# A prologue in another order, with the pooled values of block 0 as products of their own

## The chip, the cores and the metric

The kernel runs on one core of a Trainium2 chip. The metric is device time in microseconds (us), the median of several executions. The core has five engines with queues of their own: TensorE (PE, its weight loads shown as PEld), VectorE (DVE), ScalarE (ACT), GpSimd (POOL) and SyncE (SP), which here issues all transfers. Each engine works through its instructions in order and waits on semaphores where it needs another's result.

## What is computed

An attention over 4 batches, 8 heads, 768 tokens and 64 dimensions, and behind it a gated feed-forward layer. Every query sees the keys within 15 places of it, and besides them 24 pooled keys, one for each 32 tokens, whose values are means:

```python
k_sum = k.reshape(B, H, nb, block, D).max(axis=3)
v_sum = v.reshape(B, H, nb, block, D).mean(axis=3)
mask_l = np.abs(pos[:, None] - pos[None, :]) < window
scores_s = scale * np.einsum('bhsd,bhnd->bhsn', q, k_sum) + np.log(block)
scores_all = np.concatenate([np.where(mask_l, scores_l, -1e9), scores_s], axis=-1)
a = softmax(scores_all)
x = np.matmul(a, np.concatenate([v, v_sum], axis=2))
g, val = x @ w_gate, x @ w_val
out = (g / (1 + np.exp(-g)) * val) @ w_out
```

Inputs are f32, except that the three weights arrive as 64-bit floats, which the kernel turns into a high and a low f32r part by bit operations.

## The kernel before

*Blocks and units.* The 3072 tokens are cut into 8 blocks of 384 (two per batch). Attention runs per block and unit, a unit being two heads (128 channels), so four units per block. For each it computes scores (`sc`), subtracts the maximum, takes the exponential, normalises (`p`), transposes (`pp`, copied to `pt`) and multiplies by the values (`xo`). Each 64 queries see a window of 96 keys and 24 pooled ones: 120 columns of scores, 120 rows of transposed weights `pt`. The layer behind it runs per block and chunk j of 128 hidden channels, 12 chunks: `gate` and `val` (12 products of 384 columns each, three for each unit: high and low parts), the activation, and `down` (nine products of 512 columns into three accumulators `acc`).

*The prologue.* The string `PROLOGUE` is a program written out by hand: every word is a step with its block, unit or chunk, and behind `=` the engines or PSUM pools that it takes (`a`, `d`, `p` for ACT, DVE, POOL in copies and subtractions; `a`, `b`, `g` for PSUM pools in scores and transposes). It covers the attention of blocks 0 and 1, the turning of all weights and the layer for block 0 and for half of block 1. Behind it a chain of order dependencies holds each engine to the order of the text. The loop for the remaining blocks follows, places fixed by `put_attention`, and its first instruction on each engine except SP is held behind the last of the prologue. On SP a scheduler may place later transfers among the prologue's.

*Steps named below.* `kq` and `q1` load keys and queries, `cst` the constants, `ve`, `vr` and `vo` rows of values into `vrows`, `w_load` weights. `sw` makes the scores of near keys (`a_near`), `sp` those of pooled keys (`a_far`), `pool` the pooled keys `ks`; `ttr`, `exp`, `rcp`, `nrm` are the softmax, `tr` the transposes (`a_turn`), `pt` their copies, `out` the products with the values, `split` and `rest` the two parts of x. Weights go through `w_abs`, `w_c1`, `w_c2`, `w_s1`, `w_s2`, `w_hi`, `w_lo`; activations through `silu`, `mul`, `ah` (high part), `al` (low part).

*Pooled values of the first batch.* `fv` forms partial sums over the value rows in four column strips (`pv`), `fvs` copies them, `fv2` joins them by one product (`pw`), `fvc` copies the 24 joined rows to `vsum["all"]`. `spv(k)` then transfers them from there into rows 96 to 119 of six places of `vrows`, once for block 0 and once for block 1, so that `out` is one product over 120 rows for each head and 64 queries.

*Dummies.* Before the first step three products of zeros run (`WARM`), 4 + 4 + 1 pieces of 128 columns, and at four places `keep(n)` runs one of n pieces into a bank that nobody reads. An f32 product is issued as two instructions, as the counts of the profile show.

Of the kernel before, what the change touches and what calls it, by code (L numbers as in the profile page):

```python
# [78 lines left out]
exp0(0,1) w_abs(0,v) ttr1(0,1) exp1(0,1) q1() sp(0,0) ttr0(0,0) keep(4)=g sw(1,0)=aa kq(2) ttr1(0,0) exp0(0,0)  # L79
w_c1(0,v) w_c2(0,v) w_s1(0,v) rcp(0,1) w_s2(0,v) vr() sp(1,0) nrm(0,1)=p ttr0(1,0) ttr1(1,0) sw(1,1)=bb  # L80
exp1(0,0) rcp(0,0) exp0(1,0) sp(1,1)=h ttr0(1,1) nrm(0,0)=p kq(3) exp1(1,0) ttr1(1,1) sw(0,2)=ab pool(3)
keep(4)=g exp1(1,1) tr0(0,1)=b pt0(0,1)=a sw(0,3)=gb rcp(1,0) pool(2) sp(0,3) tr0(0,0)=g ttr0(0,3) sp(0,2)
nrm(1,0)=p exp0(1,1) rcp(1,1) w_hi(0,v)=d tr1(0,1)=a nrm(1,1)=p ttr0(0,2) ttr1(0,2) exp0(0,3) ve() pt1(0,1)=d
ttr1(0,3) fv()=a exp0(0,2) fvs()=a tr0(1,0)=a pt0(1,0)=d w_load(0,g) w_abs(0,g) w_load(1,gv) sw(1,2)=ab
w_c1(0,g) fv2()=g w_c2(0,g) sp(1,2) tr1(1,0)=b sw(1,3)=ab exp1(0,2) fvc()=a w_s1(0,g) vo(0) rcp(0,2) ttr0(1,2)
w_lo(0,v)=p nrm(0,2)=p w_abs(1,gv) spv(0) pt0(0,0)=d vo(1) pt1(1,0)=a ttr1(1,2) tr0(1,1)=a exp1(0,3) w_s2(0,g)
rcp(0,3) exp1(1,2) nrm(0,3)=p spv(1) sp(1,3)=h w_c1(1,gv) tr1(0,0)=g pt1(0,0)=a tr1(1,1)=a w_hi(0,g)=a
tr0(0,2)=g tr1(0,2)=b w_lo(0,g)=p w_load(2,o) out(0,1)=b ttr0(1,3) ttr1(1,3) pt0(0,2)=d split(0,1)=a pt1(0,2)=a
out(0,0)=g split(0,0)=a exp0(1,2) tr0(0,3)=b tr1(0,3)=a rest(0,1) out(0,2)=b rest(0,0) gate(0,0,0) pt0(0,3)=d
w_load(1,o) gate(0,0,1) w_load(0,o) w_c2(1,gv) val(0,0,0) w_load(2,gv) pt1(0,3)=a out(0,3)=b rcp(1,2) out(1,0)=b  # L90
w_s1(1,gv) exp0(1,3) val(0,0,1) split(0,2)=a rest(0,2) exp1(1,3) split(0,3)=d pt0(1,1)=a w_s2(1,gv) rcp(1,3)
val(0,0,2) pt1(1,1)=a split(1,0)=d rest(0,3) w_hi(1,gv)=a gate(0,0,2) out(1,1)=b nrm(1,2)=p w_abs(0,o)
tr0(1,2)=a rest(1,0) tr1(1,2)=a pt0(1,2)=a pt1(1,2)=d nrm(1,3)=p gate(0,0,3) tr0(1,3)=a tr1(1,3)=b w_c1(0,o)
w_lo(1,gv)=d val(0,0,3) silu(0,0) split(1,1)=a w_c2(0,o) w_s1(0,o) w_load(3,gv) w_abs(2,gv) mul(0,0) w_s2(0,o)
w_abs(1,o) w_c1(1,o) out(1,2)=b w_c1(2,gv) split(1,2)=a pt0(1,3)=a pt1(1,3)=d gate(0,1) w_c2(1,o) val(0,1)
out(1,3)=a room(0) silu(0,1) rest(1,1) w_load(6,o) w_c2(2,gv) w_abs(2,o) gate(1,0,0) mul(0,1) gate(1,0,1)
w_hi(0,o)=a w_abs(3,gv) val(1,0,0) rest(1,2) split(1,3)=a rest(1,3) ah(0,0)=a w_load(4,o) w_load(6,gv)
gate(1,0,2) w_s1(1,o) al(0,0)=d ah(0,1)=a al(0,1)=d w_s2(1,o) w_hi(1,o)=a w_load(3,o) w_c1(2,o) w_lo(0,o)=p
gate(1,0,3) silu(1,0) w_s1(2,gv) w_lo(1,o)=d w_load(4,gv) val(1,0,1) w_load(5,gv) val(1,0,2) val(1,0,3)
w_c2(2,o) w_abs(3,o) w_load(5,o) w_s2(2,gv) down(0,0) mul(1,0) w_c1(3,gv) w_s1(2,o) w_hi(2,gv)=a w_lo(2,gv)=d  # L100
gate(1,1) silu(1,1) w_abs(4,gv) w_c2(3,gv) val(1,1) mul(1,1) w_s1(3,gv) w_load(7,gv) w_s2(3,gv) gate(0,2)
w_c1(3,o) w_c1(4,gv) w_c2(4,gv) w_s1(4,gv) down(0,1) ah(1,1)=a al(1,1)=p gate(1,2) ah(1,0)=a al(1,0)=p down(1,0)
w_s2(2,o) w_abs(5,o) w_load(10,gv) w_hi(3,gv)=a w_lo(3,gv)=d w_c2(3,o) silu(0,2) w_hi(2,o)=a w_lo(2,o)=d
val(1,2) w_c1(5,o) w_s2(4,gv) silu(1,2) mul(1,2) val(0,2) mul(0,2) down(1,1) w_hi(4,gv)=a w_lo(4,gv)=d
w_abs(5,gv) w_c1(5,gv) ah(0,2)=a al(0,2)=d val(1,3) w_c2(5,gv) w_s1(3,o) gate(1,3) w_s2(3,o) w_load(8,o)
w_s1(5,gv) down(0,2) ah(1,2)=a w_abs(6,gv) w_c1(6,gv) w_load(9,gv) silu(1,3) mul(1,3) al(1,2)=d w_hi(3,o)=a
w_abs(4,o) gate(0,3) w_lo(3,o)=d w_load(10,o) w_c2(6,gv) w_abs(6,o) w_s2(5,gv) ah(1,3)=a al(1,3)=d w_s1(6,gv)
w_s2(6,gv) w_c2(5,o) w_c1(6,o) w_c1(4,o) silu(0,3) w_s1(5,o) gate(1,4) silu(1,4) w_hi(5,gv)=a w_hi(6,gv)=a
w_c2(4,o) w_s1(4,o) w_lo(5,gv)=d down(1,2) w_s2(4,o) w_s2(5,o) val(0,3) mul(0,3) w_c2(6,o) w_abs(9,gv)
w_c1(9,gv) val(1,4) mul(1,4) w_hi(5,o)=a w_lo(5,o)=d ah(0,3)=a w_hi(4,o)=a w_s1(6,o) down(1,3) w_lo(4,o)=d  # L110
w_abs(8,o) w_c2(9,gv) al(0,3)=p w_s2(6,o) w_lo(6,gv)=d w_s1(9,gv) gate(0,4) w_c1(8,o) ah(1,4)=d val(0,4)
silu(0,4) mul(0,4) down(0,3) w_hi(6,o)=d w_abs(7,gv) al(1,4)=d w_s2(9,gv) gate(0,5) val(0,5) w_hi(9,gv)=a
down(1,4) w_c2(8,o) w_c1(7,gv) ah(0,4)=a w_load(7,o) w_c2(7,gv) w_load(8,gv) al(0,4)=p silu(0,5) mul(0,5)
ah(0,5)=a w_s1(7,gv) w_s1(8,o) gate(0,6) w_s2(7,gv) w_lo(9,gv)=d val(0,6) w_hi(7,gv)=a w_lo(7,gv)=d al(0,5)=d
silu(0,6) w_abs(8,gv) w_s2(8,o) w_c1(8,gv) w_c2(8,gv) gate(1,5) w_abs(10,gv) silu(1,5) w_c1(10,gv) down(0,4)
mul(0,6) w_load(9,o) val(1,5) ah(0,6)=d down(0,5) w_c2(10,gv) w_s1(10,gv) w_lo(6,o)=d w_hi(8,o)=a w_abs(7,o)
w_lo(8,o)=p w_s2(10,gv) w_abs(10,o) w_abs(9,o) w_hi(10,gv)=a w_s1(8,gv) mul(1,5) w_c1(10,o) w_c1(9,o) w_c1(7,o)
w_c2(10,o) gate(0,7) al(0,6)=p w_c2(7,o) down(0,6) w_s1(10,o) ah(1,5)=a silu(0,7) w_s2(8,gv) val(0,7)
w_hi(8,gv)=a mul(0,7) w_s1(7,o) w_lo(8,gv)=d w_s2(7,o) w_c2(9,o) w_lo(10,gv)=d al(1,5)=p gate(0,9) silu(0,9)
down(1,5) w_s1(9,o) room(1) gate(0,8) ah(0,7)=a al(0,7)=d w_load(11,g) w_hi(7,o)=a w_s2(9,o) w_load(11,v)  # L120
silu(0,8) val(0,8) w_lo(7,o)=d mul(0,8) w_abs(11,g) down(0,7) w_s2(10,o) w_hi(10,o)=d val(0,9) ah(0,8)=a
al(0,8)=d down(0,8) w_lo(10,o)=p w_c1(11,g) w_hi(9,o)=d w_lo(9,o)=d w_abs(11,v) w_load(11,o) load(2,0)
w_c2(11,g) w_c1(11,v) w_c2(11,v) w_abs(11,o) w_s1(11,v) mul(0,9) w_s1(11,g) w_s2(11,g) w_s2(11,v) ah(0,9)=a
al(0,9)=d w_hi(11,g)=a gate(0,10) w_hi(11,v)=d w_c1(11,o) val(0,10) w_c2(11,o) down(0,9) w_lo(11,g)=p silu(0,10)
w_lo(11,v)=d w_s1(11,o) mul(0,10) ah(0,10)=d gate(0,11) silu(0,11) val(0,11) w_s2(11,o) al(0,10)=p down(0,10)
w_hi(11,o)=a mul(0,11) w_lo(11,o)=p ah(0,11)=a al(0,11)=d down(0,11)
"""


# [8 lines left out]
def body(ctx, tc, qP, kP, vT, vP, kq, q1, vE, vR, vO, wgv, wo, cst_in, out):  # L138
    nc = tc.nc
# [247 lines left out]
    def a_near(k, u):  # L387
        t = U[k, u]
        t["sc"] = [a_bank(k, u, f"sc{h}", on[h]) for h in range(2)]
        a = k % HALVES * TOK  # L390
        for i in range(NT):
            c, s = divmod(i, 2)
            qs = slice(i * QT, (i + 1) * QT)
            for h in range(2):
# [1 line left out]
                nc.tensor.matmul(
                    t["sc"][h][s * QT : (s + 1) * QT, c * KC : c * KC + KW], t["q"][hs, qs],
                    KT[u][hs, a + i * QT : a + i * QT + KW], start=True, stop=True,
                )

    def a_far(k, u):
        t = U[k, u]
        m = P if on == "h" else QT
        for i in range(TOK // m):
            c, s = divmod(i * m, P)
            for h in range(2):
                hs = slice(h * D, (h + 1) * D)
                nc.tensor.matmul(  # L408
                    t["sc"][h][s : s + m, c * KC + KW : (c + 1) * KC], t["q"][hs, i * m : (i + 1) * m], ksum[u][hs, :],
                    start=True, stop=True,  # L410
                )
# [56 lines left out]
        a_scale(k, u)  # L468

    def a_turn(k, u, g):  # L470
        ps = U[k, u][f"pp{g}"] = a_bank(k, u, f"pp{g}", on or "a")
        for c in range(NT // 2):
            nc.tensor.transpose(ps[:KC, c * P : (c + 1) * P], U[k, u]["p"][:, g * NT // 2 + c, :], id_sb)  # L473

# [123 lines left out]

    stack, vn = {}, {}

    def keep(n):
# [2 lines left out]
        nc.tensor.matmul(t[:, : n * P], warm[:, :P], warm[:, : n * P], start=True, stop=True)  # L604
# [41 lines left out]
    nc.vector.memset(warm, 0.0)
# [131 lines left out]
```

## Time and profile before

| what | us |
|---|---|
| median of 3 runs | 716.59 |
| lowest and highest of them | 716.12, 975.61 |
| the profiled execution | 713.79 |
| its span, first to last instruction | 712.0 |
| TensorE busy | 702.0 |
| VectorE busy | 279.6 |
| ScalarE busy | 309.1 |
| GpSimd busy | 151.3 |

The times in the views are those of the profiled execution, counted from the start of its span. A row of the timeline gives start, duration, engine, line of the code, operation, output and input, shape and count; in brackets stands how long the engine was idle before it and what ended that. `120*64` is the part of TensorE's array that a product uses, rows by columns. The highest of the three runs is a single one far from the other two.

### The profile page before, as it was taken

How to read it: one execution, taken by the hardware profiler on the slowest of the kernel's cores; microseconds unless marked ns; L12 is line 12 of the kernel's file. 1: busy time of each engine (PE TensorE's matmuls, PEld its weight loads, DVE VectorE, ACT ScalarE, POOL GpSimd, SP SyncE). 2: the span in 40 equal slices, each digit the busy share in tenths (PEclk: the TensorE clock that was granted, in tenths of full speed). 3: DMA queues.
4: the chain of work that ended last, by engine and by line, in shares of the span. 5: the costliest groups of instructions: out<-in, count | busy, mean ns of one | idle time of the engine just before them, and what ended most of it. 6: DMA issues, size and time to landing. Idle time of an engine off the chain costs nothing.

```text
span 712.0 us, 12729 instructions
## 1 busy us (share of the span) xinstructions
PE 702.0 (99%) x5106; PEld 638.6 (90%) x5106; DVE 279.6 (39%) x814; ACT 309.1 (43%) x763; POOL 151.3 (21%) x151
## 2 busy tenths in 40 slices
...
GB/s 340 226 377 417 130 1 0 131 75 186 163 169 67 46 43 2 112 46 91 90 58 77 68 46 46 46 72 18 46 46 45 89 17 1 1 45 1 1 1 44
DMA packets 49123, 61.93 MB, mean 87 GB/s; under 512 B 20968, under 2 KB 38120, under 8 KB 47784
## 3 DMA queue, kind: packets, MB, share of 16 engines
...
q8 instruction: 40, 0.66, 0.4%
q14 instruction: 19, 0.16, 0.1%
...
## 4 chain that ended last, share of the span: by engine, by line
PE 94%; ACT 2%; DVE 2%; DMA 1%; issue 0%; POOL 0%; ACTq 0%
PE v L535 29%; PE g L535 28%; PE acc L585 28%; PE xo L500 4%; PE sc L381 3%; PE pp L473 2%; DMA vrows<-vs 1%; PE dummy L604 1%; DVE p L422 1%; ACT p L437 0%; PE pv L348 0%; DVE ks L294 0%; PE pv L330 0%; POOL al L158 0%; ACT L437 0%
## 5 line engine op out<-in xcount | busy, mean ns | idle before, releaser
L535 PE MATMUL v<-xh,w_gv 128*128 128x384 f32 x640 | 179.3, 341 | 0.0
L585 PE MATMUL acc<-w_o,ah 128*128 128x512 f32 x576 | 178.9, 392 | 0.0
L535 PE MATMUL g<-xh,w_gv 128*128 128x384 f32 x640 | 178.6, 340 | 0.0
L158 POOL TENSOR_TENSOR al<-a,ah 128x384 fp32r<-128x384 f32 x84 | 89.3, 1063 | 313.3 <-ACT ah L162 309.7
L546 DVE TENSOR_TENSOR a<-v,a 128x384 f32<-128x384 f32 x96 | 53.4, 556 | 253.9 <-PE v L535 252.8
L585 PEld LDWEIGHTS acc<-w_o,ah 128*128 128x128 f32 x576 | 108.0, 188 | 19.7
L535 PEld LDWEIGHTS v<-xh,w_gv 128*128 128x128 f32 x640 | 117.2, 188 | 3.4 <-issue 2.4
L535 PEld LDWEIGHTS g<-xh,w_gv 128*128 128x128 f32 x640 | 117.3, 188 | 2.6 <-ACT a L541 0.3
L585 PE MATMUL acc<-w_o,al 128*128 128x512 f32 x288 | 113.6, 395 | 0.1
L541 ACT ACTIVATE a<-g 128x384 f32<-128x384 f32 x96 | 47.1, 491 | 143.8 <-PE g L535 142.3
L535 PE MATMUL g<-xl,w_gv 128*128 128x384 f32 x320 | 108.0, 338 | 0.0
L535 PE MATMUL v<-xl,w_gv 128*128 128x384 f32 x320 | 107.9, 337 | 0.0
L162 ACT CAST ah<-a 128x384 fp32r<-128x384 f32 x93 | 47.3, 510 | 112.5 <-DVE a L546 105.4
L437 ACT ACTIVATE p<-p,nm 128x120 f32<-128x120 f32 x192 | 73.2, 383 | 6.9 <-DVE nm L422 6.7
L459 POOL TENSOR_TENSOR p<-p,ri 128x720 f32<-128x720 f32 x32 | 45.8, 1432 | 121.3 <-DVE ri L455 107.1
L585 PEld LDWEIGHTS acc<-w_o,al 128*128 128x128 f32 x288 | 54.0, 188 | 9.9 <-issue 0.5
L535 PEld LDWEIGHTS g<-xl,w_gv 128*128 128x128 f32 x320 | 60.1, 188 | 2.3
L535 PEld LDWEIGHTS v<-xl,w_gv 128*128 128x128 f32 x320 | 60.1, 188 | 0.3
L541 ACT ACT_TABLE_LOAD x25 | 32.1, 1283 | 53.0 <-PE g L535 52.9
L422 DVE CUSTOM_DVE_ANT_0 p<-sc,consts 128x120 f32<-128x120 f32 x192 | 41.3, 277 | 1.7 <-PE sc L408 1.4
L535 PE MATMUL g<-xh,w_g 128*128 128x384 f32 x128 | 36.9, 345 | 0.0
L535 PE MATMUL v<-xh,w_v 128*128 128x384 f32 x128 | 36.6, 343 | 0.0
...
## 6 DMA issues: line engine op xcount, KB each, us to landing
...
```

What stands on the lines that cost most here:

```text
L158: (nc.vector if e == "d" else nc.gpsimd).tensor_tensor(out=out, in0=a, in1=b.bitcast(F32), op=ALU.subtract)
L162: nc.scalar.copy(out, in_)
L381: nc.tensor.matmul(sc[h][s * QT : (s + 1) * QT, c * KC : (c + 1) * KC], t["q"][hs, qs], t["kw"][hs, i, :], start=True, stop=True,)
L422: nc.vector.tensor_tensor_reduce(out=t["p"][:, i, :], in0=t["sc"][g][:, c * KC : (c + 1) * KC], in1=bias_sb[:, 0 if n == 0 else 2 if n == ...
L437: nc.scalar.activation(out=t["p"][:, i, :], in_=t["p"][:, i, :], func=AF.Exp, scale=-1.0, bias=t["nm"][:, i : i + 1], accum_out=t["sm"][:, ...
L459: (nc.vector if on == "d" else nc.gpsimd).tensor_tensor(out=p, in0=p, in1=ri.rearrange("p (n o) -> p n o", o=1).broadcast_to([P, NT, KC]), ...
L473: nc.tensor.transpose(ps[:KC, c * P : (c + 1) * P], U[k, u]["p"][:, g * NT // 2 + c, :], id_sb)
L500: nc.tensor.matmul(ps[hs, qs], vw, t["pt"][:n, h, qs], start=k not in OWN or i == 0, stop=k not in OWN)
L535: nc.tensor.matmul(ps[:, :TOK], w[:, cs], x, start=u == 0 and n == 0, stop=u == NP - 1 and n == 2)
L541: nc.scalar.activation(out=a, in_=A.pop(("g", k, j))[:, :TOK], func=AF.Silu)
L546: nc.vector.tensor_tensor(out=a, in0=ps[:, :TOK], in1=a, op=ALU.mult)
L585: nc.tensor.matmul(ACC[k][i], a[:, ts], w, start=j == 0 and n == 0, stop=j == NJ - 1 and n == 2)
```

## The change

Five things change. (1) `WARM` goes from (4, 4, 1) to (4, 3), into one bank. (2) The `keep` steps go; instead a score step can begin with a product of zeros into its own bank (`zeros`), of as many 128-column pieces as the digit behind its pools says. (3) `OWN = (0,)`: for block 0 `out` multiplies only the 96 rows of near values, in one accumulation, and a new use of `outp` adds the 24 pooled rows as one product of 384 columns per head; `spv(0)` goes. (4) Transfers behind the prologue's are held behind its last one, too. (5) The text of the prologue is written in a new order, with other engines for some copies.

```diff
-WARM = (4, 4, 1)
-OWN = ()
+WARM = (4, 3)
+OWN = (0,)
...
     def a_near(k, u):
...
         t["sc"] = [a_bank(k, u, f"sc{h}", on[h]) for h in range(2)]
+        zeros(t["sc"][0], on[2:])
...
     def a_far(k, u):
         t = U[k, u]
-        m = P if on == "h" else QT
+        m = P if on[:1] == "h" else QT
+        for _ in range(int(on.strip("hq") or 0)):
+            nc.tensor.matmul(t["sc"][0][:, NTP * P :], warm[:, :P], warm[:, :P], start=True, stop=True)
...
     def a_turn(k, u, g):
-        ps = U[k, u][f"pp{g}"] = a_bank(k, u, f"pp{g}", on or "a")
+        ps = U[k, u][f"pp{g}"] = a_bank(k, u, f"pp{g}", on[:1] or "a")
+        zeros(ps, on[1:])
...
-    def keep(n):
-
-        t = a_bank(0, 0, "dummy", on)
-        nc.tensor.matmul(t[:, : n * P], warm[:, :P], warm[:, : n * P], start=True, stop=True)
+    def zeros(t, n):
+
+        if n:
+            nc.tensor.matmul(t[:, : int(n) * P], warm[:, :P], warm[:, : int(n) * P], start=True, stop=True)
...
-        if x.engine in last and x.engine != mybir.EngineType.SP:
+        if x.engine in last:
             after(x, last[x.engine])
```

`a_out` and `a_out_pooled` are in both kernels; before, `OWN` was empty and no step called the second:

```python
n = KW if k in OWN else KC
...
nc.tensor.matmul(ps[hs, qs], vw, t["pt"][:n, h, qs], start=k not in OWN or i == 0, stop=k not in OWN)
...
vw = vsum["all"][KW:, u * P + h * D : u * P + (h + 1) * D]
nc.tensor.matmul(t["xo"][hs, :TOK], vw, t["pt"][KW:, h, :], start=False, stop=True)
```

The first line of the text, before and after. Zero products stand in `sw(0,1)`, `sp(0,1)` and, further on, `sw(0,3)=ga3`: 4, 1 and 3 pieces.

```diff
-kq(1) sw(0,1)=ag keep(2)=a pool(1) kq(0) keep(2)=b cst() pool(0) sp(0,1) sw(0,0)=ga ttr0(0,1) w_load(0,v)
+kq(0) cst() sw(0,0)=bg kq(1) pool(0) q1() w_load(0,g) sp(0,0) ttr0(0,0) exp0(0,0) sw(0,1)=bg4 pool(1) sp(0,1)=h1
```

Over the whole prologue the new text gives DVE 15 `al` instead of 11, 5 `ah` instead of 3, the `fvc` copy, 11 low parts of single weights instead of 9, 5 `pt` instead of 7 and 1 `split` instead of 2.

SyncE's queue before, from the last rows of values on (`vrows<-vs` is a spread, `vw` are value windows of block 2):

```order
L178 DMA raw_gv_426<-in_wgv 128x2048
L630 DMA vrows<-in_vO 128x1536
L286 DMA vw_0_1853<-in_vP 96x6x128
L286 DMA vw_1_1948<-in_vP 96x6x128
L370 DMA vrows<-vs_479 24x6x512
L630 DMA vrows<-in_vO 128x1536
L370 DMA vrows<-vs_479 24x6x512
L178 DMA raw_o_546<-in_wo 128x1024
```

The same place after:

```order
L249 DMA kq_262<-in_kq 128x1184
L627 DMA vrows<-in_vE 128x2x1536
L177 DMA raw_v_409<-in_wgv 128x1024
L633 DMA vrows<-in_vO 128x1536 x2
L177 DMA raw_gv_519<-in_wgv 128x2048
L369 DMA vrows<-vs_521 24x6x512
L177 DMA raw_o_552<-in_wo 128x1024
```

Both rows of `vO` and the first double chunk now stand ahead of the only spread, and the two windows of block 2 have left the place.

TensorE's order before, from the transposes of unit 2 to the first gate product (`xo_1_548` is unit 1 of block 0):

```order
L473 MATMUL pp_0_2_541<-consts,p_2_386 120x128 x3
L500 MATMUL xo_1_548<-pt_1_318,vrows 64x64 x12
L500 MATMUL xo_0_577<-pt_0_497,vrows 64x64 x12
L473 MATMUL pp_0_3_596<-consts,p_3_354 120x128 x3
L473 MATMUL pp_0_3_600<-consts,p_3_354 120x128 x3
L500 MATMUL xo_2_605<-pt_2_571,vrows 64x64 x12
L535 MATMUL g_0_619<-xh_0_590,w_g_535 128x384
```

And after, from the join of the partial sums (`pw`) to the first gate product:

```order
L359 MATMUL pw_0_490<-warm,consts 120x512
L476 MATMUL pp_0_2_502<-consts,p_2_356 120x128 x3
L503 MATMUL xo_0_506<-pt_0_264,vrows 64x64 x12
L511 MATMUL xo_0_506<-pt_0_264,vs_521 64x384 x2
L503 MATMUL xo_1_534<-pt_1_454,vrows 64x64 x12
L476 MATMUL pp_0_2_547<-consts,p_2_356 120x128 x3
L476 MATMUL pp_0_3_568<-consts,p_3_399 120x128 x3
L511 MATMUL xo_1_534<-pt_1_454,vs_521 64x384 x2
L538 MATMUL g_0_578<-xh_0_557,w_g_476 128x384
```

The pooled products of units 0 and 1 (`vs`, 384 columns) have come between, and the first gate product stands ahead of the values of units 2 and 3.

More of the change, by code (lines that the diff above doesn't have):

```diff
@@ L77 @@
 PROLOGUE = """
-kq(1) sw(0,1)=ag keep(2)=a pool(1) kq(0) keep(2)=b cst() pool(0) sp(0,1) sw(0,0)=ga ttr0(0,1) w_load(0,v)
[L79 to L126, printed above, removed]
+kq(0) cst() sw(0,0)=bg kq(1) pool(0) q1() w_load(0,g) sp(0,0) ttr0(0,0) exp0(0,0) sw(0,1)=bg4 pool(1) sp(0,1)=h1
@@ new lines @@
+kq(2) sw(1,0)=aa ttr1(0,0) exp1(0,0) sp(1,0) ttr0(0,1) vr() rcp(0,0) ttr1(0,1) exp0(0,1) sw(1,1)=bb w_abs(0,g)
+ttr0(1,0) ttr1(1,0) sp(1,1)=h nrm(0,0)=p exp1(0,1) tr0(0,0)=g exp0(1,0) kq(3) pt0(0,0)=a exp1(1,0) tr1(0,0)=b
+ttr0(1,1) w_c1(0,g) rcp(0,1) nrm(0,1)=p w_c2(0,g) pool(2) ttr1(1,1) sw(0,2)=gb sw(0,3)=ga3 pool(3) pt1(0,0)=a
+ve() w_s1(0,g) rcp(1,0) sw(1,2)=ab sp(0,2)=h sp(1,2)=h w_s2(0,g) exp0(1,1) ttr0(0,2) ttr1(0,2) exp1(1,1) sp(0,3)
+tr0(0,1)=b tr1(0,1)=g exp0(0,2) nrm(1,0)=p tr0(1,0)=a rcp(1,1) ttr0(0,3) ttr1(0,3) w_load(0,v) vo(0) tr1(1,0)=b
@@ new lines @@
+exp1(0,2) fv()=g ttr0(1,2) exp0(0,3) nrm(1,1)=p tr0(1,1)=a pt0(1,0)=a tr1(1,1)=a rcp(0,2) ttr1(1,2) fvs()=a
+pt0(0,1)=d pt1(0,1)=d vo(1) exp1(0,3) pt1(1,0)=d sw(1,3)=ba w_hi(0,g)=d sp(1,3) fv2()=b rcp(0,3) nrm(0,2)=p
+ttr0(1,3) tr0(0,2)=g out(0,0)=b w_load(1,gv) fvc()=d spv(1) w_abs(0,v) outp(0,0) exp0(1,2) w_c1(0,v) nrm(0,3)=p
+w_c2(0,v) out(0,1)=g tr1(0,2)=b w_lo(0,g)=d w_load(0,o) exp1(1,2) split(0,0)=a pt0(0,2)=a w_abs(1,gv) rcp(1,2)
+rest(0,0) pt1(0,2)=d tr0(0,3)=b ttr1(1,3) outp(0,1) nrm(1,2)=p gate(0,0,0) w_s1(0,v) w_load(1,o) w_c1(1,gv)
@@ new lines @@
+tr1(0,3)=b w_s2(0,v) out(0,2)=b outp(0,2) exp0(1,3) pt0(0,3)=a pt1(0,3)=a out(1,0)=b w_hi(0,v)=a w_c2(1,gv)
+pt0(1,1)=a split(0,2)=d out(0,3)=b rest(0,2) split(0,1)=a outp(0,3) w_load(3,o) w_abs(0,o) pt1(1,1)=a tr0(1,2)=b
+w_load(2,gv) rest(0,1) w_lo(0,v)=p w_s1(1,gv) w_s2(1,gv) val(0,0,0) val(0,0,1) split(1,0)=a out(1,1)=a exp1(1,3)
+rcp(1,3) tr1(1,2)=a gate(0,0,1) split(0,3)=a w_hi(1,gv)=a gate(0,0,2) rest(0,3) rest(1,0) nrm(1,3)=p gate(0,0,3)
+w_load(5,o) val(0,0,2) val(0,0,3) w_c1(0,o) w_c2(0,o) w_lo(1,gv)=d pt0(1,2)=a pt1(1,2)=a tr0(1,3)=b w_s1(0,o)
@@ new lines @@
+w_s2(0,o) silu(0,0) split(1,1)=a w_abs(2,gv) out(1,2)=b tr1(1,3)=a mul(0,0) w_hi(0,o)=a w_load(2,o) w_c1(2,gv)
+rest(1,1) w_lo(0,o)=p ah(0,0)=a pt0(1,3)=a gate(0,1) al(0,0)=p silu(0,1) split(1,2)=a w_load(3,gv) pt1(1,3)=d
+val(0,1) w_c2(2,gv) w_abs(2,o) out(1,3)=b w_abs(1,o) val(1,0,0) mul(0,1) rest(1,2) w_s1(2,gv) w_c1(2,o)
+split(1,3)=a val(1,0,1) rest(1,3) w_c2(2,o) w_load(4,gv) room(0) w_abs(3,gv) gate(1,0,0) gate(1,0,1) val(1,0,2)
+ah(0,1)=a al(0,1)=d val(1,0,3) gate(1,0,2) w_c1(1,o) gate(1,0,3) down(0,0) w_load(7,gv) w_c2(1,o) w_s1(1,o)
@@ new lines @@
+w_abs(3,o) silu(1,0) mul(1,0) w_s2(1,o) ah(1,0)=a gate(1,1) w_c1(3,gv) w_s2(2,gv) w_s1(2,o) w_hi(1,o)=a
+w_load(5,gv) w_lo(1,o)=d w_load(10,gv) w_load(10,o) al(1,0)=d w_hi(2,gv)=a w_s2(2,o) w_c1(3,o) w_c2(3,gv)
+w_lo(2,gv)=d silu(1,1) val(1,1) mul(1,1) w_load(8,gv) w_abs(4,gv) w_hi(2,o)=d down(0,1) w_lo(2,o)=d w_c1(4,gv)
+w_c2(3,o) w_s1(3,gv) w_s2(3,gv) w_s1(3,o) ah(1,1)=a w_load(4,o) gate(0,2) silu(0,2) w_hi(3,gv)=a al(1,1)=d
+w_c2(4,gv) gate(1,2) w_s2(3,o) w_abs(4,o) w_c1(4,o) val(0,2) mul(0,2) silu(1,2) w_abs(10,o) down(1,0)
```

28 lines of the change are left out of this document (25 added, 3 removed).

## The prediction

> **What bounds the kernel now.** I read the page's busy table first, then the stages, then TensorE's timeline and the chain of waits in the first 45 us. In the stages (below the page's two lines) the columns are the stretch, the busy time and instructions of PE, PEld, DVE, ACT and POOL, the granted clock, the DMA share and GB/s.
>
> ```profile
> span 712.0 us, 12729 instructions
> PE 702.0 (99%) x5106; PEld 638.6 (90%) x5106; DVE 279.6 (39%) x814; ACT 309.1 (43%) x763; POOL 151.3 (21%) x151
> ...
> 0.00:10.00 10.00, 7.89 (x107) 5.00 (x108) 4.05 (x20) 2.62 (x8) 0.20 (x4) 1.00 0.79 290
> 10.00:20.00 10.00, 9.17 (x203) 5.77 (x204) 9.51 (x60) 10.00 (x51) 5.06 (x4) 1.00 1.03 409
> 20.00:30.00 10.00, 8.39 (x117) 4.88 (x111) 8.72 (x50) 8.74 (x31) 5.18 (x5) 1.00 0.87 230
> 30.00:40.00 10.00, 8.55 (x138) 7.79 (x139) 6.47 (x13) 5.87 (x25) 3.29 (x2) 0.83 0.66 197
> 40.00:100.00 60.00, 59.91 (x379) 55.80 (x378) 55.73 (x85) 33.49 (x53) 7.13 (x5) 1.00 0.62 255
> 100.00:157.00 57.00, 57.00 (x296) 52.82 (x296) 46.91 (x74) 20.70 (x34) 12.80 (x8) 1.00 0.14 45
> 700.00:712.00 12.00, 8.23 (x42) 7.19 (x40) 2.23 (x4) 1.96 (x4) 0.18 (x1) 1.00 0.18 66
> ```
>
> TensorE sets the time: 702.0 of 712.0 us. Of the 10 us in which it is idle, 6.0 lie in the first 40 us and 3.8 in the last 12, which the change leaves alone. So the end moves by when TensorE starts, by the products added and removed, and by the holes of the first 40 us. Its timeline there (start, duration, what, count, idle time before it and what ended that):
>
> ```profile
> 1.45 4.21 PE L604 MATMUL dummy<-warm 128*128 128x512 f32 x6 [1.45 <-DVE warm L646]
> 5.59 1.16 PE L396 MATMUL sc<-kq 64*64 64x96 f32 x24
> 6.68 1.13 PE L604 MATMUL dummy<-warm 128*128 128x256 f32 x4
> 7.74 0.55 PE L408 MATMUL sc<-ks,kq 64*64 64x24 f32 x24
> 8.11 0.70 PE L396 MATMUL sc<-kq 64*64 64x96 f32 x24
> ...
> 9.79 1.10 PE L604 MATMUL dummy<-warm 128*128 128x512 f32 x2 [0.66 <-DVE nm L422]
> 11.16 0.73 PE L396 MATMUL sc<-kq,q 64*64 64x96 f32 x24 [0.28 <-DMA q<-in_q]
> ...
> 12.66 0.85 PE L408 MATMUL sc<-ks,q 64*128 64x24 f32 x12
> ...
> 14.10 1.12 PE L604 MATMUL dummy<-warm 128*128 128x512 f32 x2
> 15.61 0.52 PE L473 MATMUL pp<-consts,p 128*120 128x128 f32 x3 [0.39 <-DVE nm L422]
> ...
> 19.01 2.88 PE L348 MATMUL pv<-vrows,consts 128*32 128x512 f32 x14
> ...
> 30.83 2.83 PE L500 MATMUL xo<-pt,vrows 120*64 120x64 f32 x48 [2.44 <-DMA vrows<-vs]
> ...
> 34.50 0.92 PE L500 MATMUL xo<-pt,vrows 120*64 120x64 f32 x24
> 35.35 0.44 PE L535 MATMUL g<-xh,w_g 128*128 128x384 f32 x1
> 35.63 0.34 PE L535 MATMUL g<-xl,w_g 128*128 128x384 f32 x1
> ...
> 38.67 0.92 PE L500 MATMUL xo<-pt,vrows 120*64 120x64 f32 x24 [0.62 <-DMA vrows<-vs]
> ```
>
> The holes after the start are 0.66, 0.28, 0.39, 2.44 and 0.62 us: 4.39 together. The last two wait for the transfers that spread the pooled values over the value rows. They are on the chain of waits (first two lines), SyncE holds the weight loads behind them (next three), and behind the first hole the granted clock stands at 0.50 for 3 us (last line, columns as in the stages):
>
> ```profile
> 25.89 4.80 DMA vrows<-vs
> 32.97 5.56 DMA vrows<-vs
> ...
> 11.13 4.01 SPq L286 DMA_DIRECT2D vw<-in_vP  x2
> 25.89 0.98 SPq L370 DMA_DIRECT2D vrows<-vs  x1
> 33.81 2.71 SPq L178 DMA_DIRECT2D raw_o<-in_wo  x3
> ...
> 30.83:33.85 3.02, 3.02 (x49) 2.90 (x50) 1.07 (x2) 1.01 (x3) 0.28 (x1) 0.50 0.28 114
> ```
>
> **The change, part by part.** *Start: -0.94 us.* Nine zero blocks of 128 columns took 4.21 us, seven take 3.27, so the first scores come at 4.72 instead of 5.66. Their keys are there, since the first reduction over keys starts at 4.54:
>
> ```profile
> 4.54 0.95 DVE L294 TENSOR_REDUCE ks<-kq 128x24 f32<-128x768 f32 x1 [3.14 <-DMA kq<-in_kq]
> ```
>
> *Dummies out, zero products in: -3.35 and +2.24.* The dummies behind the start took 1.13 + 1.10 + 1.12 us. The new zero products are 4 + 1 + 3 blocks at 1.12 / 4 = 0.28 each. They run ahead of scores, on TensorE's path.
>
> *Own products for the pooled values: +4.0, from 2.5 to 7.4.* Each unit of block 0 gets two products of 384 columns, over 24 rows and into 64 columns, each issued as two instructions like the other f32 ones. No row has this shape. A full f32 instruction of 512 columns takes 1.12 / 2 = 0.56 us, so one of 384 takes 0.42. Four in a row make 1.68 per unit, with a switch 1.85 (upper end, x4 = 7.4). If the two heads run side by side in the two column halves it is 0.84. The cheapest near row is pv, which uses column strips: 14 instructions of 512 columns in 2.88 us, 0.21 each, hence 4 x 0.21 x 384/512 = 0.62 (lower end, x4 = 2.5). The scores come nearer in kind, 64-wide tiles of both heads in turn: 24 instructions of 96 columns in 0.70 us are 0.029 each, where a full array would take 0.56 x 96/512 = 0.105, so 3.6 of 4 tiles worked at once. I take 0.84 plus 0.16, 1.0 per unit, for switches: the first g behind the 64-wide xo takes 0.44 us and the next 0.34, so one costs 0.10. The remaining products keep their count and width; 96 rows instead of 120 are costed at nothing.
>
> The Trainium skill, TensorEngine Tiling (Array Packing), section Tiling Modes, speaks against these products: a change of tiling mode drains TensorE. The trace agrees as far as its 0.10 us goes. Without any drain the products would come to 4 x 0.84 = 3.4 and the sum below to 0.6 us less.
>
> *Holes: -3.3, and the slow clock: -1.2.* Block 0 waits for no spread any more: -2.44. The second spread (block 1) is issued when the joined sums are copied. Between the join and the first product that needs it TensorE has four pp (0.5 each), three out (0.85), three pooled products (1.0) and a gate piece (0.5): 8.1 us. The copy of 24x512 (0.58 in the row below) and 4.80 to 5.56 of transfer are 6.1 at most: -0.62, with 2 us to spare. The queries of block 1 go ahead of one 512 KB weight, 1.3 us at 409 GB/s, and arrive at 9.9; TensorE is there at 4.72 + 1.16 + 0.55 + 1.12 + 0.70 + 0.28 + 0.85 = 9.4. That is a hole of 0.5, the 0.39 may stay, and of the three small ones (1.33) I leave 1.1. Behind the hole of 2.44 us 48 xo took 2.83 us where 2 x 0.85 was due; the stage at a clock of 0.50 lasted 3.02 us, and I put the loss at 1.2. No hole of such a length is left.
>
> *Transfers.* Block 2's two value windows leave the prologue's queue, 4.01 us of SyncE's time, and come behind block 0's results. They are needed at 172.08, and results leave at 155.60; even the slowest spread above took 5.56 us, so it is hidden, and without that cover TensorE would wait for the difference. Only one spread is left, issued some 2 us after the place of the old first one (25.89), so the weights behind it start at about 28.5 instead of 33.81.
>
> *DVE: +0.4, from 0 to 3.7.* It gets four more low parts of activations (0.55 each), one cast more (0.55 at most), the copy of the pooled values (0.58) and two more low parts of weights (0.73), less two copies of turned weights (0.55): +3.7. That is hidden as long as TensorE is the later one: from 40 us on DVE waits for a product 7.3 us in five waits. But the low part of the third weight chunk ends at 59.32 + 1.22 = 60.54 and block 0's gate with it starts at 61.47 (the g row below), so there the cover is 0.9 us.
>
> ```profile
> L158 DVE TENSOR_TENSOR al<-a,ah 128x384 fp32r<-128x384 f32 x11 | 6.0, 551 | 0.6 <-ACT ah L162 0.6
> L158 DVE TENSOR_TENSOR w_o<-m_o,w_o 128x512 fp32r<-128x512 f32 x8 | 5.8, 728 | 0.0
> L162 ACT COPY vs<-pw 24x512 f32<-24x512 f32 x1 | 0.6, 579 | 0.0
> ...
> DVE a L546 <- PE v L535: 7.3, 5, 2.5
> ...
> 59.32 1.22 DVE L158 TENSOR_TENSOR w_gv<-m_gv,w_gv 128x1024 fp32r<-128x1024 f32 x1
> 61.47 0.34 PE L535 MATMUL g<-xh,w_gv 128*128 128x384 f32 x1
> ...
> 155.60 1.69 SPq L596 DMA_DIRECT2D out<-o  x3
> 172.08 0.96 DVE L164 COPY vw<-vs 24x768 f32<-24x768 f32 x1 [0.16 <-ACT vs L331]
> ```
>
> The sum: -0.94 - 3.35 + 2.24 + 4.0 - 3.3 - 1.2 + 0.4 = -2.15 us. The profiled execution took 713.79 us, 1.8 around its span; it would take 711.6. It lies 2.8 under the median of the runs, 716.59. The forecast is for the median: 714.4 us.
>
> **The rivals.** *The wait moves on* (the change does not do what it says). The first pooled product stands behind one pp and one out (1.35 us) after the join, and needs the copy (0.58), which is now DVE's: 0.8 us to spare. If DVE, in order, comes to that copy 3 us late, a hole of 2.2 us and the slow clock's 1.2 are back: -2.15 + 3.4 = +1.25, 717.8 us. For it: DVE is busy 9.5 and 8.7 of 10 us in the stages from 10 to 30. Against it: its work ahead of the copy is scores that TensorE has long delivered. Chance 0.13.
>
> *The pooled products run one behind the other*: 7.4 in place of 4.0, -2.15 + 3.4 = +1.3, 717.9 us. For it: both heads read the same 24 rows, where the scores' heads read different ones. Against it: pv's strips share their rows too and come to 0.21 us. Chance 0.12.
>
> *DVE takes over, slower than before.* The place is the gate of block 0's third weight chunk. TensorE gets there at about 61.0, 2.5 us sooner by the sum but with a down product of 2.1 us put ahead of it. By the order DVE has 1.4 us more to do before it, against a cover of 0.9. So TensorE waits unless DVE is idle at least 1 us less before than it was: 0.5 + 1.3 + 3.5 us in the stages from 10 to 40. If DVE keeps the lead in time from there on, none of TensorE's gain comes through and the extra work shows in full: 716.6 + 3.7 = 720.3 us. For it: DVE is busy 55.73 of 60 us. Against it: 3.5 of that idle time lies in the stage of the spread's holes, and the weights arrive 5 us sooner. Chance 0.14.
>
> *The slow clock at the start lasts longer.* The first scores take 1.16 us and the next ones 0.70, so the clock comes up at about 6.5 us. If it comes one stage of 3 us later, work of that stage takes twice the time: -2.15 + 1.5 = -0.65, 715.9 us. For it: seven zero blocks instead of nine, then smaller tiles. Against it: TensorE has no hole there before 9.4. Chance 0.08. The Trainium skill, TensorE: Matmul & The Clock Gate, Part 1: The HAM clock gate, has a rule for this: a window of about 3.4 us that runs freely decides, so the moment of the rise varies between executions. The trace has one rise and one fall and agrees with the length, 3.02 us; it can't show the variation.
>
> *Cheaper than reckoned*: pooled products at 2.5, no small hole left: -2.15 - 1.5 - 1.1 - 0.4 = -5.1, 711.5 us. Chance 0.06.
>
> **How the numbers follow.** The forecast has 0.47 and is the predicted time. Its own range is 712 to 717, from 2.5 to 5 for the pooled products and 0 to 1.5 for DVE. The range for 8 in 10 is 710.5 to 719.0: it takes in the cheap case and three of the rivals, and leaves out most of DVE's. Two per cent, 14.3 us, is about what a measurement of this kernel can tell from no change. A gain of that size would need all idle time, all dummies and the start together, so faster gets 0.01. A loss of it needs weights to be late by four times DVE's extra work: 0.03, out of the DVE rival. The rest, 0.96, is within 2%.
>
> **What would show it.** Each step has its row in the changed profile: first scores at 4.7 us; pooled products at 1.0 us per unit; no wait of xo for the spread; no stage at a clock of 0.50 after 7 us; the first gate about 3 us sooner than 35.35; PE busy up by about 2 us and idle time down by 3. The forecast is wrong if TensorE waits for DVE at gates between 40 and 150 us, if the pooled products take 1.7 us per unit, or if a hole of over 2 us opens ahead of them.

## The result, and the profile after

| | us |
|---|---|
| the changed kernel, median of 6 runs | 710.8 (710.54 to 711.5) |
| the kernel before, median of 6 runs | 715.08 (713.18 to 975.61) |
| ratio of the runs, 95% interval | 0.9946 (0.9929 to 0.9964) |
| profiled execution, before and after | 713.79 and 711.5 |
| span, before and after | 712.0 and 709.7 |

The change makes the kernel 0.54% faster, some 4 us by this comparison: clear of noise, and within the 2% for which 0.96 was given. Forecast were 714.4 us, in 710.5 to 719.0. The measured median lies 0.3 us above the lower end of that range. The two profiled executions differ by 2.3 us, where the sum of the prediction said 2.15. Single executions far above the rest, like the 975.61 here, do not enter a ratio.

The page of the changed kernel, then its stages, columns as before:

```profile
span 709.7 us, 12696 instructions
PE 702.5 (99%) x5094; PEld 638.6 (90%) x5094; DVE 281.2 (40%) x820; ACT 308.7 (43%) x763; POOL 140.2 (20%) x145
...
20.00:30.00 10.00, 10.00 (x139) 5.77 (x139) 8.65 (x46) 8.76 (x36) 5.13 (x4) 1.00 0.64 231
30.00:40.00 10.00, 10.00 (x136) 7.54 (x133) 9.05 (x21) 8.29 (x25) 3.07 (x3) 1.00 0.96 355
40.00:100.00 60.00, 60.00 (x360) 56.41 (x360) 55.99 (x89) 30.46 (x47) 3.93 (x3) 1.00 0.52 215
100.00:157.00 57.00, 57.00 (x298) 53.10 (x297) 47.16 (x73) 20.75 (x33) 5.93 (x5) 1.00 0.15 48
157.00:200.00 43.00, 42.19 (x370) 36.52 (x369) 25.61 (x84) 29.04 (x78) 13.04 (x15) 1.00 0.71 204
```

TensorE's busy time rises by 0.5 us and its idle time falls from 10.0 to 7.2. From 16 to 157 us it has no hole at all, and the clock stays at 1.00 where it had been 0.83. One stage is worse: from 157 to 200 us TensorE is idle for 0.81 us, against 0.12 before, as the same stage of the kernel before shows:

```profile
157.00:200.00 43.00, 42.88 (x373) 38.26 (x372) 25.87 (x84) 28.57 (x77) 12.24 (x15) 1.00 0.61 184
```

The timeline of TensorE in the changed kernel, at the places that answer to those shown of before, and with the hole of block 2 at its end:

```profile
4.74 1.24 PE L396 MATMUL sc<-kq 64*64 64x96 f32 x24
5.75 0.80 PE L410 MATMUL sc<-ks,kq 64*64 64x24 f32 x24
6.48 1.49 PE L607 MATMUL sc<-warm 128*128 128x512 f32 x2
8.20 0.73 PE L396 MATMUL sc<-kq 64*64 64x96 f32 x24 [0.23 <-DMA kq<-in_kq]
8.86 0.49 PE L405 MATMUL sc<-warm 128*128 128x128 f32 x2
9.27 0.85 PE L410 MATMUL sc<-ks,kq 64*128 64x24 f32 x12
10.09 0.73 PE L396 MATMUL sc<-kq,q 64*64 64x96 f32 x24
...
12.76 0.87 PE L476 MATMUL pp<-consts,p 128*120 128x128 f32 x6 [0.32 <-DVE nm L424]
...
14.99 0.91 PE L607 MATMUL sc<-warm 128*128 128x384 f32 x2 [0.56 <-ACT pt L161]
...
26.52 0.92 PE L503 MATMUL xo<-pt,vrows 96*64 96x64 f32 x24
27.37 0.86 PE L511 MATMUL xo<-pt,vs 24*64 24x384 f32 x4
28.16 0.92 PE L503 MATMUL xo<-pt,vrows 96*64 96x64 f32 x24
...
30.60 0.44 PE L538 MATMUL g<-xh,w_g 128*128 128x384 f32 x1
...
33.30 1.62 PE L503 MATMUL xo<-pt,vrows 120*64 120x64 f32 x48
...
172.90 0.51 PE L476 MATMUL pp<-consts,p 128*120 128x128 f32 x3 [0.81 <-DVE nm L424]
```

A pooled product starts at 27.37 and the next instruction at 28.16: 0.79 us per unit. The first product that needs a spread (block 1, at 33.30) has no wait before it. SyncE's queue and VectorE's waits show why, and what the hole of block 2 hangs on (timelines; the last line is from the waits from 157 to 200 us, with total, times and longest):

```profile
27.02 0.98 SPq L369 DMA_DIRECT2D vrows<-vs  x1
28.05 2.65 SPq L177 DMA_DIRECT2D raw_o<-in_wo  x3
...
162.35 0.95 DVE L314 TENSOR_REDUCE vr<-vt 128x24 f32<-128x768 f32 x1 [2.48 <-DMA vt<-in_vT]
...
DVE vr L314 <- DMA vt<-in_vT: 3.0, 2, 2.5
```

The spread leaves at 27.02, the weights behind it at 28.05 instead of 33.81. In block 2, values of unit 1 stand behind the queries and key windows of the same unit, which the change has put behind the results; VectorE, in order, waits 2.48 us for them. The chain of waits of this execution leads from that transfer, issued at 156.73, over this reduction and further work of VectorE and ScalarE to the transposes at 172.90.

### The profile page after: what moved, and what is told of

It is laid out like the page before. It is cut to its first block, busy times and chain, and to the rows that moved or that the text cites. A ratio compares the mean times of both kernels' runs of the same rounds, so it can differ in the third digit from the quotient of the medians.

```text
span 709.7 us, 12696 instructions
## 1 busy us (share of the span) xinstructions
PE 702.5 (99%) x5094; PEld 638.6 (90%) x5094; DVE 281.2 (40%) x820; ACT 308.7 (43%) x763; POOL 140.2 (20%) x145
## 4 chain that ended last, share of the span: by engine, by line
PE 94%; DMA 2%; ACT 2%; DVE 1%; SPq 0%; issue 0%
PE v L538 28%; PE g L538 28%; PE acc L588 27%; PE xo L503 4%; PE pp L476 3%; PE sc L380 2%; ACT p L439 1%; DMA kq<-in_kq 1%; DMA vt<-in_vT 1%; PE xo L511 0%; PE pv L347 0%; DVE ks L293 0%; PE sc L410 0%; PE sc L396 0%; PE pv L329 0%
## 5 line engine op out<-in xcount | busy, mean ns | idle before, releaser
L157 POOL TENSOR_TENSOR al<-a,ah 128x384 fp32r<-128x384 f32 x80 | 81.5, 1019 | 300.8 <-ACT ah L161 300.8
```

What stands on the lines that cost most here:

```text
L157: (nc.vector if e == "d" else nc.gpsimd).tensor_tensor(out=out, in0=a, in1=b.bitcast(F32), op=ALU.subtract)
```

## The experiments

Twelve runs in three groups. In each group the kernel before ran on the same chip: medians 713.95, 714.43 and 714.08 us. Times and ratios below are against that. A ratio is worked out from the single executions, so it can differ by 0.1% from the quotient of the two medians. "The changed kernel" is the one of the change; its own second measurement is the fifth run.

### Later transfers free again

```diff
-        if x.engine in last:
+        if x.engine in last and x.engine != mybir.EngineType.SP:
```

> The changed kernel without its fourth part: later transfers may again be placed among the prologue's by the scheduler. Theory (the ledger: every part is worth what its rows show on TensorE's path): the hold costs the one hole that the changed kernel has in block 2, 0.81 us at 172.9, where VectorE had waited 2.48 us for a transfer of values. Freed, queries and windows of unit 1 leave before the results again, the hole closes, and the kernel is 0.5 to 0.8 us faster than the changed one (about 710.1 against 710.8). Rival: the hold is part of the gain, because the two value windows of block 2 now go among the last weights and delay them; then it is the same or slower by up to 1 us.

710.63 us, ratio 0.9958 (0.9943 to 0.9973). The scheduler puts the two value windows among the last weights, and the queries of unit 1 ahead of the results. The hole of block 2 closes to 0.13 us, as the stage of this run shows:

```profile
157.00:200.00 43.00, 42.87 (x408) 37.41 (x406) 26.29 (x86) 29.53 (x79) 13.02 (x15) 1.00 0.58 171
```

In this order, the hole was the hold's doing. Whether the time falls with it, this pair alone does not tell: the intervals of this ratio and the changed kernel's overlap almost wholly. For the rival, a delay by the windows, nothing speaks: they leave at 59.19 us, and the time is no longer.

### Block 0's spread put back

```diff
-OWN = (0,)
+OWN = ()
...
-out(0,0)=b w_load(1,gv) fvc()=d spv(1) w_abs(0,v) outp(0,0)
+w_load(1,gv) fvc()=d spv(0) out(0,0)=b spv(1) w_abs(0,v)
```

The other three `outp` go as well.

> The changed kernel with the pooled values of block 0 spread by a transfer again, in the new order: no own products. Theory: it saves the four pairs of products (4 x 0.79 = 3.2 us) and gets back a hole behind the join, because the copy ends near 27.0 us, a spread takes 4.8 and TensorE has only some 1.3 us of transposes between; hole 3 to 5 us, clock at 0.50 for up to 3.4 us behind it (1 to 1.7 lost). Net 1 to 3.5 us slower than the changed kernel. Rival: the new order alone makes the gain, then this one is as fast as the changed kernel or up to 3 us faster.

715.69 us, ratio 1.002 (1.0011 to 1.0028): 4 to 5 us slower than the changed kernel, and slower than the kernel before. TensorE's wait and the two stages around it in this run:

```profile
31.89 2.83 PE L503 MATMUL xo<-pt,vrows 120*64 120x64 f32 x48 [5.01 <-DMA vrows<-vs]
...
20.00:30.00 10.00, 6.88 (x82) 3.43 (x80) 7.81 (x44) 7.36 (x35) 4.87 (x4) 0.97 0.58 217
30.00:40.00 10.00, 7.44 (x132) 7.01 (x132) 4.94 (x14) 5.23 (x15) 1.35 (x2) 0.69 0.95 305
```

That is more than expected: the hole is 5.01 us, at the top of its range. The clock column gives the time at half clock: what is missing to 1.00, times the length of the stage, times two. Here that is (0.03 + 0.31) x 10 x 2 = 6.8 us, twice the 0.17 x 10 x 2 = 3.4 of the kernel before. With a spread for block 0 at this place, the new order alone is worth less than nothing.

### Without the zero products

```diff
-sw(0,1)=bg4
+sw(0,1)=bg
-sp(0,1)=h1
+sp(0,1)=h
-sw(0,3)=ga3
+sw(0,3)=ga
```

> The changed kernel without its three zero products. Theory: they take 2.7 us on TensorE (1.49, 0.41 and 0.84), but two of them only fill waits: the second keys land at 8.18 in any case, and the bank of the third is free at 14.99. So 0.4 to 1.2 us faster than the changed kernel, the small holes grow to 2.5 us together, and the clock stays at 1.00 after its rise. Rival (the clock needs them): a hole of 1.5 us at 6.5 us keeps the clock at 0.50 for one more stage of 3.4 us, so 0.5 to 1.5 us slower than the changed kernel, with a granted clock below 1.00 in the stage from 7 to 14 us.

712.83 us, ratio 0.9993 (0.9976 to 1.0011): 1.4 to 2.0 us slower than the changed kernel's two medians, 711.43 and 710.8. TensorE's timeline, then the stages of this run:

```profile
7.14 0.72 PE L396 MATMUL sc<-kq 64*64 64x96 f32 x24 [0.85 <-DMA kq<-in_kq]
8.13 0.85 PE L410 MATMUL sc<-ks,kq 64*128 64x24 f32 x12 [0.27 <-DVE ks L293]
9.11 1.15 PE L396 MATMUL sc<-kq,q 64*64 64x96 f32 x24
...
0.00:10.00 10.00, 7.30 (x112) 4.79 (x116) 4.65 (x24) 4.22 (x16) 0.20 (x4) 0.96 0.78 298
10.00:20.00 10.00, 9.95 (x200) 8.70 (x192) 8.53 (x54) 8.86 (x42) 4.47 (x3) 0.70 1.01 407
```

The theory fell, the rival held. Behind two holes of 0.85 and 0.27 us the scores take 1.15 us where they took 0.73, and the clock is at half for 6.8 us ((0.04 + 0.30) x 20). In ten of the twelve executions the mean clock is 0.995 or less. The other two, at 0.999 and 1.000, took 712.91 and 717.68, so the clock does not explain every execution.

### Only the first zero product

The second and the third are taken out as above, `sw(0,1)=bg4` stays.

> The changed kernel without its second and third product of zeros (1 and 3 pieces); the first of 4 pieces stays. Theory: without all three the clock fell because the wait for the second keys lay open within its first full stage; the first product covers that wait, the others only cost their 0.41 and 0.84 us, less what opens as waits. So 0.5 to 1.2 us faster than the changed kernel, clock at 1.00 from its rise on. Rival: the small ones are needed as well, then the clock is at 0.50 for a stage between 6 and 20 us and it is 0.5 to 2 us slower.

714.79 us, ratio 0.9997 (0.9981 to 1.0013); single times from 711.9 to 717.4, but for one far off. That is 3.4 us slower than the changed kernel beside it, 711.43, and more than the rival said. Again the theory fell. In the profile the wait that the third product had stood in lies open, and the clock falls a little later:

```profile
15.56 0.73 PE L396 MATMUL sc<-kq 64*64 64x96 f32 x24 [1.08 <-ACT p L439]
...
10.00:20.00 10.00, 8.31 (x205) 7.36 (x206) 9.63 (x62) 9.94 (x50) 4.46 (x3) 0.89 1.02 403
20.00:30.00 10.00, 10.00 (x109) 5.80 (x107) 6.04 (x39) 6.04 (x27) 3.76 (x3) 0.77 0.53 215
```

The single executions agree: three with a mean clock of 1.000 took 711.9 to 712.6 us, eight with 0.996 or less 712.9 to 717.4. So the products of zeros are paid for by the clock that they keep, the second and third too, which were taken out together; which of these two it needs is not shown.

### The kernel before without its dummies

Every `keep(n)` is taken out of the text.

> The kernel before without its four dummies. Theory of the prediction: they are on TensorE's path, 3.35 us, of which some 1.1 turn into a wait for the queries: 1.5 to 2.5 us faster than before. Rival (from the run without zero products): they keep the clock up, without them it falls to 0.50 for one or two stages in the first 20 us, and the kernel is the same or up to 2 us slower.

716.44 us, ratio 1.0016 (1.0002 to 1.0029): slower by about 1 to 2 us, not faster by 2: the rival held. The wait for the queries lies open, and the clock is at half for 13.6 us ((0.44 + 0.24) x 20):

```profile
11.24 1.33 PE L396 MATMUL sc<-kq,q 64*64 64x96 f32 x24 [3.54 <-DMA q<-in_q]
...
10.00:20.00 10.00, 8.76 (x162) 7.58 (x162) 7.79 (x41) 8.71 (x45) 4.44 (x3) 0.56 1.02 407
20.00:30.00 10.00, 10.00 (x123) 4.47 (x123) 6.04 (x35) 6.09 (x22) 3.17 (x3) 0.76 0.68 189
```

### Own products alone in the kernel before

```diff
-OWN = ()
+OWN = (0,)
```

`spv(0)` goes and each `out(0,u)` is followed by `outp(0,u)`.

> The kernel before with the own products alone: no spread for block 0, each out of block 0 followed by its pooled product; order, dummies and all else as before. Theory: the hole of 2.44 goes with its slow clock (1.2), the hole of 0.62 goes or shrinks, and the products cost 4 x 0.79 = 3.2: about 1 us faster than before (0.5 to 2). Rival (the order is what counts): no gain or slower by up to 1.5 us, because TensorE only runs into the next wait of the old order, for transposed weights or weights of the layer.

713.0 us, ratio 0.999 (0.9978 to 1.0002). Its profile was of an execution at a clock of 0.85 throughout, so it was run once more for the rows:

> The kernel before with own products alone, once more, for a profile at full clock. Theory: no wait of xo for the spread, no stage at a clock of 0.50 behind it, pooled products 0.79 us per unit; the first gate product at about 35 us as before the change, since 3 products have come ahead of it; the median about 1 us under the kernel before. Rival: the clock falls elsewhere, or the wait moves to block 1's spread.

712.92 us, ratio 0.9993 (0.9981 to 1.0006). The stages of the second profile:

```profile
20.00:30.00 10.00, 10.00 (x147) 5.90 (x140) 8.69 (x50) 8.73 (x31) 5.13 (x5) 1.00 0.91 271
30.00:40.00 10.00, 10.00 (x134) 7.35 (x132) 7.00 (x15) 7.07 (x26) 3.58 (x3) 1.00 0.96 341
```

The holes of the spread and the slow clock are gone, as expected; the first gate product comes at 34.03, 1 us sooner than expected. Both medians lie 1 us under the kernel before, as the ledger says (2.44 + 0.62 + 1.2 - 3.2), but both intervals include no change. The size fits; that there is a gain is not shown by the times alone.

### Own products for block 1 too

```diff
-OWN = (0,)
+OWN = (0, 1)
```

`spv(1)` goes and each `out(1,u)` is followed by `outp(1,u)`.

> The changed kernel with own products for block 1 too, and no spread at all. Theory: own products pay where a spread is waited for and only there. In the changed order block 1's spread is covered (no wait of TensorE for it), so four more pairs at 0.79 us are lost: 2 to 3.5 us slower than the changed kernel, about 713.5, with the clock at 1.00. Rival: the spread still costs, through 1 us of SyncE's queue and a late start of the weights; then it is within 1 us of the changed kernel.

713.96 us, ratio 0.9998 (0.9988 to 1.0008), 2.5 to 3.2 us slower than the changed kernel's two medians, 711.43 and 710.8. Four pairs at 0.79 are 3.2. The two profiled spans, 712.1 and 709.7, differ by 2.4. That fits 3.2 less the 0.81 of block 2's hole, which is not there this time, though VectorE waits 2.47 us for the values again. The last row below shows that; those before it, TensorE's holes at the start and the stage behind them, bear on the clock:

```profile
5.60 0.55 PE L410 MATMUL sc<-ks,kq 64*64 64x24 f32 x24 [0.26 <-DVE ks L293]
8.10 0.73 PE L396 MATMUL sc<-kq 64*64 64x96 f32 x24 [0.90 <-DMA kq<-in_kq]
...
10.00:20.00 10.00, 9.11 (x223) 7.80 (x222) 9.81 (x65) 10.00 (x51) 4.60 (x4) 1.00 1.02 404
...
157.00:200.00 43.00, 43.00 (x372) 37.99 (x371) 25.32 (x83) 28.60 (x77) 12.31 (x15) 1.00 0.75 208
```

Holes of about the length of those in the run without zero products, with the first zero product between them, left the clock at 1.00. Where the spread is covered, the products only cost.

### The hold alone in the kernel before

```diff
-        if x.engine in last and x.engine != mybir.EngineType.SP:
+        if x.engine in last:
```

> The kernel before with its later transfers held behind the prologue's, and nothing else. Theory: block 2's value windows leave the prologue, which frees 4 us of SyncE's queue that nobody waited for, since the first spread is issued when the sums are copied; and block 2 gets the changed kernel's hole of 0.5 to 0.8 us. So 0 to 1 us slower than before. Rival: the windows' 0.58 MB held up the first spread; then the hole of 2.44 shrinks to about 1 us and the kernel is 1 to 2 us faster.

712.85 us, ratio 0.9978 (0.9967 to 0.999): 1.2 us faster by the medians. Here the theory fell and the time is the rival's. TensorE's two waits at the spread, and SyncE's issue of the first, in this run:

```profile
30.14 1.62 PE L500 MATMUL xo<-pt,vrows 120*64 120x64 f32 x48 [1.33 <-DVE nm L422]
37.38 0.92 PE L500 MATMUL xo<-pt,vrows 120*64 120x64 f32 x24 [1.33 <-DMA vrows<-vs]
...
25.27 0.98 SPq L370 DMA_DIRECT2D vrows<-vs  x1
```

The spread leaves 0.62 us sooner, at 25.27 instead of 25.89, and the first hole shrinks from 2.44 to 1.33. The profile puts its end down to VectorE, which is done at 30.11; a transfer of 4.80 us as before would land at 30.07, so which of the two ended the hole is not settled. The second hole grows from 0.62 to 1.33. After neither does the clock fall: 48 xo take 1.62 us where they took 2.83. The hole of block 2 did not come: in this order VectorE's wait for the values, 2.27 us, stays covered.

How the gain comes is not shown, though. This execution was the slowest of its eleven, and its span is 711.9 us against 712.0: what TensorE has won by 40 us it loses again in two waits for ScalarE that the kernel before does not have.

```profile
43.74 0.92 PE L500 MATMUL xo<-pt,vrows 120*64 120x64 f32 x24 [0.30 <-ACT pt L162]
45.55 0.45 PE L535 MATMUL g<-xh,w_gv 128*128 128x384 f32 x1 [0.88 <-ACT a L541]
```

### Only the value windows held

```diff
+        windows.update(id(x) for x in traced[n:])
...
-        if x.engine in last:
+        if x.engine in last and (x.engine != mybir.EngineType.SP or id(x) in windows):
```

`windows` collects the transfers of `a_load_values`. The changed kernel stood beside it:

> The changed kernel itself once more, beside the others of this group, as their common measure. About 710.8 us. Its hole in block 2 (0.81 us) should be there again, and the clock at 1.00 from its rise on; the moment of the rise may differ between executions by up to one window of some 3.4 us, as 4.7, 5.2 and 7.4 us in three profiles of the changed order so far.

> The changed kernel with only block 2's value windows held behind the prologue's transfers; all other later transfers free for the scheduler, as before the change. Theory: the hole of block 2 came from queries and key windows of unit 1 that were held, so it closes, and nothing goes among the weights: 0.5 to 0.8 us faster than the changed kernel. Rival: the transfers behind the results are late in any case, then it is within 0.2 us of the changed kernel.

The changed kernel: 711.43 us, ratio 0.9955 (0.9938 to 0.9972), single times 710.15 to 712.2; its hole in block 2 is 0.54 us this time, its clock 1.00 again. With the windows held: 710.46 us, ratio 0.9939 (0.9924 to 0.9955), 709.67 to 710.78 but for one execution of 1763 us, which the profile happened to be of. So it was run again:

> The kernel with only block 2's value windows held, once more, for a profile (the first one was of a disturbed execution) and more times. Theory: TensorE's idle time from 157 to 200 us falls from 0.5 to 0.8 in the changed kernel to about 0.1, VectorE no longer waits some 2.5 us for a transfer of values there, and the median stays near 710.4, 0.5 us below the changed kernel's. Rival: the hole is there again, and the median within the changed kernel's range of 710.2 to 712.2.

710.34 us (710.17 to 710.83), ratio 0.9954 (0.994 to 0.9967). TensorE is busy without a break in block 2's stage. VectorE still waits 1.24 us for the values there, half of what it did, where about nothing was expected:

```profile
157.00:200.00 43.00, 43.00 (x412) 37.80 (x410) 26.27 (x85) 29.52 (x79) 12.96 (x15) 1.00 0.66 189
```

With the run that frees all later transfers this shows that, in the new order, the hold opens the hole. A gain of some 0.7 us would fit its size: the mean of twelve times of the changed kernel is 711.1, of ten with the windows held 710.35. But the ratios' intervals overlap, and all transfers free gave 710.63, so no version is shown to be the best.

## Why the prediction was right, point by point

*TensorE bounds, and the first 40 us decide.* Right. But the split was not: the terms add up to +1.7 us of busy time and -3.8 of idle time (the prediction's own list says +2 and -3), and measured were +0.5 and -2.8.

*Start, -0.94.* Right: first scores at 4.74 instead of 5.59, -0.85.

*Dummies out, zero products in, -3.35 and +2.24.* The net, -0.6 instead of -1.1, was near (the new ones take 1.49 + 0.41 + 0.84 = 2.74 from start to start), but the reason was wrong. I counted both as mere cost. Without the dummies the old kernel was slower, without the zero products the new one lost 1.4 to 2.0 us: what they cost is less than what the clock would cost without them. That the exchange came out near the forecast is luck: both sets keep the clock up, and the prediction did not ask for that.

*Own products, +4.0.* Mis-sized: 0.79 per unit, 3.2 in all. The two heads do run side by side (0.84 was that case), and the 0.16 for switches was not to be seen. The drain that the Trainium skill, TensorEngine Tiling (Array Packing), section Tiling Modes, names is not visible at this place: instructions of the two shapes stand at 0.85 and 0.79 from start to start.

*Holes, -3.3.* Right for the first 40 us: 0.23 + 0.32 + 0.56 = 1.11 is left of 4.39, and 1.1 was forecast. Which small holes stay came out otherwise: the queries are there in time, and it is the second keys, at 8.20, that TensorE waits for. The 0.81 us of block 2 were not in the term.

*Slow clock, -1.2.* Right that it goes. That the hole of the spread can bring it is shown by the run that puts the hole back, where the clock falls for 6.8 us, and by the run with own products alone, where hole and slow clock go together in the profile. It is not the only cause: in five of the twenty undisturbed executions of that kernel the mean clock is still 0.993 or 0.994, and they took 714.5 to 716.3 us. The length was misread: 3.02 us is the window shown, all of it at 0.50, and the 0.83 of the whole stage gives 3.4.

*Transfers, nothing on the path.* Wrong, in both directions. The two value windows did stand in the spread's way: with the hold alone it leaves 0.62 us sooner and the median falls by 1.2, though through which wait is not shown. And holding all later transfers costs the changed kernel a hole of 0.81 us in block 2. I looked only at whether the windows themselves would be late, not at what else the hold moves on SyncE's queue: queries, key windows and values of unit 1.

*DVE, +0.4.* Right that it stays hidden; TensorE waits for nothing between 40 and 157 us. DVE's busy time rises by 1.6 us, not by the 3.7 reckoned, so the 0.4 in the sum came to nothing.

*The rivals.* The wait did not move on, the products did not run one behind the other, DVE did not take over. A longer slow start is in the profile: the scores at 5.75 still run slowly and the 512 zeros behind them take 1.49 us instead of 1.12, but the cost stays under 1 us.

*Sum and median.* On the profiled executions the sum is near: -2.15 forecast, -2.3 measured. That it is so near is in part luck. The products came 0.8 cheaper and DVE's 0.4 fell away; against them stand 0.5 less from the exchange of the zero products and 0.7 for the longer idle time of block 2. The median missed its forecast by 3.6 us. Most of that is its base: 716.59 came from three executions, and later medians of the same kernel, of 23 to 35 executions each, are 713.95 to 714.43. From there the same sum gives 711.8 to 712.3.

Some 1 us is left, and the single executions narrow it down. Of the 85 of the kernel before in the three groups, 19 have a mean clock of 0.996 or less, with medians of 715.6 to 716.0 by group, and 36 have 1.000, with 713.8 to 713.9. So the clock falls for longer in some executions than in others, and that makes the upper part of their spread. But without a slow clock the sum would be only -0.95, and the changed kernel's own medians, all at 1.000, are 711.43 and 710.8: at full clock the kernel before is still 2.5 us slower in the group that has both. Where the other 1.5 us go is open, since no execution of before at 1.000 was profiled.
